# Block-causal attention with an RWKV channel mix: every PSUM use takes a pair of banks, the channel mix goes in pairs of blocks

## The chip, the cores and the metric

The kernel runs on one core of one Trainium2 chip. The metric is the device time of one execution in microseconds; lower is better. The engines named below are TensorE (PE, with its weight loads PEld), VectorE (DVE), ScalarE (ACT), GpSimd (POOL) and SyncE (SP). They work side by side, each through its own instructions in order, and wait for each other on semaphores.

## What is computed

Attention over 8 batches of 8 heads, 576 tokens and 64 columns per head, where a query block of 64 sees its own and earlier key blocks; then a channel mix over the 4608 tokens of 512 columns.

```python
scores = where(block_i >= block_j, q @ k.T / sqrt(64), -1e9)
x = softmax(scores) @ v                      # heads side by side: 8 x 576 x 512
x_prev = x shifted by one token
xk = mu_k * x + (1 - mu_k) * x_prev
xr = mu_r * x + (1 - mu_r) * x_prev
k = maximum(xk @ w_k, 0)                     # 512 -> 1024
v = (k * k) @ w_v                            # 1024 -> 512
out = sigmoid(xr @ w_r) * v                  # float32
```

The sigmoid is computed as a tanh: 0.5 * (1 + tanh(0.5 r)), with the 0.5 folded into w_v.

## The kernel before

The attention goes batch by batch. For each batch, `add_qk` loads q and k for four heads at a time and VectorE transposes them ("turn", L458); `add_unit` makes the scores of six units of up to 512 columns (TensorE L563; keys on partitions) into two pairs of PSUM banks, and ScalarE takes the exponential of each pair in one instruction of 1024 columns (L584). `add_av` multiplies with v: kind S sums the exponentials (L647), T, A and B are the products (L658); VectorE makes the reciprocals of the sums and normalizes into `xt` (L687, L695). `add_mix` forms xk and xr of the batch (differences on POOL, DVE or ACT, L778, L782; products on VectorE, L798, L802). Batch 0 goes in two parts of its own (`add_part`).

The channel mix goes by chunks of 512 tokens, nine in all. In chunk c, `add_pk` multiplies for one of eight column blocks jc of w_k (four matmuls of 512 columns, L834), then comes a relu into `kr` (ACT L847 or DVE L849) and a square into `k2` (ACT L856, DVE or POOL L858). `add_pr` does one of four token blocks of 128 with w_r (four matmuls, L873) and a tanh (ACT, L882). `add_pv` does one token block with w_v (eight matmuls, L903), VectorE forms (1 + tanh) * v as the output (L911), and SyncE stores 128 x 512 of it (L918). The first 192 tokens of chunk 0 go apart from its other 320.

Each of these steps is a task of a plan. `ORDER` lists the tasks by number, and that is the order in which they are issued, so the order on every engine; "+n" puts n filler matmuls ahead of a TensorE task (`unread`, L413). `PLACE` says with one letter each which engine takes a task that could go to several.

PSUM has eight banks of 512 float32 columns per partition. They are held as four tiles of two banks (`t_ps0` to `t_ps3`). Attention takes a whole tile (size 2); every k, r and v group takes one bank, that is half a tile (size 1). `take` chooses the half: first one whose neighbour is in use, then the one that was freed first in the order of issue:

```python
elif b["size"] == 1:
    at = min((ring[n ^ 1][1], s[0], n)
             for n, s in enumerate(ring) if s[1])[2]
```

Buffers behind the PSUM groups: four `kr`, four `t` and three `o`, each of 512 columns.

Of the kernel before, what the change touches and what calls it, by code (L numbers as in the profile page):

```python
# [61 lines left out]
"""  # L62

PLACE = (
    "SPSDSPADDDAAAAPAAPDDDPDPDPDPAAPPAPPDDADPAPPDPAPPDAPDPADAPPPDADAAAADDDA"
    "AAAAAPAPAPAPAPAPAPDPAAADAAAAAPAPAPAPAPAPAPDPAPAPAAAAAAADAAAPAAADAPADDA"
    "APAADDAAAAAADAAAAADADDADDPADAAAADDADAADPAAAPADADAPAPAAAAADDDDPAAAPDDAA"
    "DADAADDDADAADA")


class Plan:


    def __init__(self, rings):
        self.rings = rings
        self.slots = {n: [[i, True] for i in range(k)] for n, k in rings.items()}
        self.tasks = []
        self.issued = 0
# [925 lines left out]
```

## Time and profile before

| what | value |
|---|---|
| median of 3 runs | 299.59 us (299.56 to 302.61) |
| profiled execution: time, span | 299.6 us, 297.8 us |
| granted TensorE clock, mean | 0.966 |
| PE busy | 258.8 us (87%) |
| DVE busy | 190.6 us (64%) |
| ACT busy | 176.2 us (59%) |
| POOL busy | 74.5 us (25%) |
| chain that ended last: PE, DVE, ACT | 73%, 10%, 7% |

The span goes from the first to the last instruction of the profiled execution; its time is 1.8 us longer. Busy times of TensorE hold the matmuls' pipelined ends, so a run of matmuls counts some 0.2 us beyond its last start interval. The chain is the sequence of work that ended last: TensorE makes up three quarters of it, and the instructions that empty PSUM stand between its pieces. A timeline row gives start, length, engine, line, operation, tiles and how many instructions it merges; in brackets stands the engine's idle time ahead of it and whose end ended that.

### The profile page before, as it was taken

What the parts mean: (1) busy time and instruction counts of PE and PEld (TensorE: products, weight loads), DVE (VectorE), ACT (ScalarE), POOL (GpSimd) and SP (SyncE); (2) the same over time, 40 slices, a digit from 0 to 9 for tenths busy, and PEclk for the clock granted to TensorE, in tenths of its full rate; (3) what the DMA queues carried; (4) which work ended last, traced back from release to release, by engine and by line L of the source; (5) the groups of instructions that cost most, each with busy time, mean ns of one, the idle gap of its engine ahead of it and who ended that gap; (6) DMA issues with size and microseconds to landing.
All of it is one profiled execution on the core that took longest, in us unless ns stands there. A gap on an engine that the chain in (4) does not pass through costs nothing.

```text
span 297.8 us, 9076 instructions
## 1 busy us (share of the span) xinstructions
PE 258.8 (87%) x4056; PEld 133.5 (45%) x4056; DVE 190.6 (64%) x266; ACT 176.2 (59%) x255; POOL 74.5 (25%) x91
## 2 busy tenths in 40 slices
PE   8689489999998998998999889898988999886763
PEld 3356134753453445543544575454445644332322
DVE  0657860798787778969677768776855593452021
ACT  1077067688976787776658868866754754650101
POOL 0334320145568226313352002101030400200000
PEclk9979855999999999999999999999999999999999
DMA  7999999627999399729538600200111003001122
GB/s 167 220 210 188 194 255 267 118 34 111 212 223 206 50 237 206 133 69 235 85 53 175 155 4 2 108 35 4 37 73 37 2 0 141 2 1 51 56 78 98
DMA packets 49911, 33.75 MB, mean 113 GB/s; under 512 B 39248, under 2 KB 39504, under 8 KB 49872
## 3 DMA queue, kind: packets, MB, share of 16 engines
q1 hardware_dynamic: 44816, 22.75, 32.5%
q0 software_dynamic: 4896, 9.83, 19.8%
q10 hardware_dynamic: 160, 0.59, 0.8%
q8 instruction: 31, 0.51, 0.7%
q14 instruction: 8, 0.07, 0.1%
HBM read 33.56 MB, written 9.44 MB: 144 GB/s over the span
## 4 chain that ended last, share of the span: by engine, by line
PE 73%; DVE 10%; ACT 7%; issue 5%; DMA 3%; SPq 1%; POOL 0%; DVEq 0%; ACTq 0%; POOLq 0%
PE t_ps L834 21%; PE t_ps L903 20%; PE t_ps L873 10%; PE t_ps L563 9%; PE t_ps L658 6%; PE t_ps L413 4%; DVE t_o L911 4%; PE t_ps L647 3%; DMA t_lq<-in_q_dram 3%; ACT t_t L882 3%; ACT t_kr L847 2%; DVE t_qkt L458 2%; DVE t_kr L849 1%; ACT t_e L584 1%; DVE t_xt L695 1%
## 5 line engine op out<-in xcount | busy, mean ns | idle before, releaser
L584 ACT ACTIVATE t_e<-t_ps 128x1024 f16<-128x1024 f32 (+3 forms) x96 | 87.8, 973 | 33.4 <-PE t_ps L563 33.3
L834 PE MATMUL t_ps<-t_xk,WK 128*128 128x512 f16 (+5 forms) x416 | 69.0, 315 | 8.8 <-ACT t_kr L847 5.6
L903 PE MATMUL t_ps<-WV,t_k 128*128 128x512 f16 (+1 forms) x296 | 67.6, 373 | 9.0 <-DVE t_o L911 3.9
L834 PEld LDWEIGHTS <-WK 128*128 128x128 f16 x416 | 37.0, 98 | 36.2 <-issue 12.4
L847 ACT ACTIVATE t_kr<-t_ps 128x512 f32<-128x512 f32 (+2 forms) x61 | 31.8, 553 | 29.7 <-PE t_ps L834 17.1
L911 DVE SCALAR_TENSOR_TENSOR t_o<-t_t,t_ps 128x512 f32<-128x512 f32 (+1 forms) x37 | 24.2, 669 | 35.8 <-PE t_ps L903 26.0
L903 PEld LDWEIGHTS <-t_k 128*128 128x128 f16 x296 | 27.9, 97 | 42.8 <-issue 13.2
L858 POOL TENSOR_TENSOR t_k<-t_kr 128x512 f16<-128x512 f32 (+2 forms) x28 | 26.1, 944 | 78.1 <-DVE t_kr L849 45.3
L882 ACT ACTIVATE t_t<-t_ps 128x512 f32<-128x512 f32 x36 | 20.8, 598 | 39.6 <-PE t_ps L873 22.9
L563 PE MATMUL t_ps<-t_qkt 32*64 32x64 bf16 (+7 forms) x1328 | 40.0, 310 | 3.6 <-DVE t_qkt L458 2.9
L873 PE MATMUL t_ps<-WR,t_xr 128*128 128x512 f16 x144 | 36.1, 381 | 5.0 <-DVE t_o L911 4.3
L458 DVE STREAM_TRANSPOSE t_qkt<-t_nb 128x576 f32<-128x576 f32 x32 | 37.7, 1241 | 4.0 <-PE t_ps L563 2.2
L563 PEld LDWEIGHTS <-t_qkt 32*64 32x64 bf16 x1328 | 21.7, 111 | 27.3 <-issue 22.9
L849 DVE TENSOR_SCALAR t_kr<-t_ps 128x512 f32<-128x512 f32 (+2 forms) x19 | 12.0, 643 | 30.7 <-PE t_ps L834 17.9
L782 POOL TENSOR_TENSOR t_d<-t_xt 128x576 f32<-128x576 f32 (+2 forms) x14 | 16.6, 1188 | 56.6 <-DVE t_xr L802 21.9
L413 PE MATMUL t_ps<-identb 128*128 128x512 bf16 x72 | 22.6, 442 | 3.4 <-ACT t_e L584 1.9
L856 ACT ACTIVATE t_k<-t_kr 128x512 f16<-128x512 f32 (+2 forms) x33 | 18.9, 585 | 6.9 <-DVE t_kr L849 6.4
L873 PEld LDWEIGHTS <-t_xr 128*128 128x128 f16 x144 | 13.3, 98 | 20.6 <-issue 7.3
L802 DVE SCALAR_TENSOR_TENSOR t_xk<-t_d,MUK,t_xt 128x576 f16<-128x576 f32 (+2 forms) x26 | 21.4, 830 | 1.1 <-POOL t_d L782 1.0
L658 PE MATMUL t_ps<-t_e,t_vo 64*32 64x64 f16 (+7 forms) x1120 | 21.3, 284 | 0.8 <-issue 0.6
L695 DVE TENSOR_TENSOR t_xt<-t_ps,t_rt 128x1024 f32<-128x1024 f32 x14 | 17.0, 1222 | 6.4 <-PE t_ps L658 6.4
L802 DVE SCALAR_TENSOR_TENSOR t_xr<-t_d,MUR,t_xt 128x576 f16<-128x576 f32 (+2 forms) x26 | 19.7, 771 | 0.1
(43 smaller groups left out, 175.2 us busy)
## 6 DMA issues: line engine op xcount, KB each, us to landing
t_lv<-in_v_dram SPq DMA_DIRECT2D x32, 288.0 KB, 7.5
out_dram<-t_o SPq DMA_DIRECT2D x35, 256.0 KB, 2.2
t_nb<-in_k_dram POOLq DMA_DIRECT2D x14, 288.0 KB, 6.1
t_nb<-in_q_dram POOLq DMA_DIRECT2D x14, 288.0 KB, 6.5
t_lq<-in_moe_w_v_dram SPq DMA_DIRECT2D x4, 512.0 KB, 21.5
t_lq<-in_q_dram SPq DMA_DIRECT2D x4, 288.0 KB, 8.5
WK<-in_moe_w_k_dram POOLq DMA_DIRECT2D x4, 256.0 KB, 10.3
t_lq<-in_k_dram ACTq DMA_DIRECT2D x2, 288.0 KB, 5.3
```

The lines of the kernel that those rows point to most:

```text
L413: nc.tensor.matmul(dst, identb, identb[:, :].unsqueeze(1).to_broadcast([P, 4, P]), start=True, stop=True)
L458: nc.vector.transpose(new(qkt)[:, n, g].rearrange("p t e -> p (t e)").bitcast(FP).rearrange("p (r j) -> p j r", r=RW), new(nb)[:, :].bitca ...
L563: nc.tensor.matmul(new(ms[a // 2])[y * D:y * D + D, a % 2, col:col + n], qkt[rows, 1, g, t * D:t * D + D, f], qkt[rows, 0, g, q0:q0 + n, f ...
L584: nc.scalar.activation(new(e)[:, 2 * h:2 * h + 2, 0:w], new(ms[h])[:, :, 0:w], AF.Exp, scale=ISQ)
L658: nc.tensor.matmul(PA[o, u, HALF + f * D:HALF + f * D + D] if kind == "T" else PA[o, u, lo - D:lo - D + n], weight(b, u, c, t % JT, f), E[ ...
L802: e.scalar_tensor_tensor(dst, dt[:, 0, 0:W], (MUK1, MUR1)[n][:, cc:cc + 1], x, ALU.mult, ALU.add)
L834: nc.tensor.matmul(ps[:, a:a + n], WK[:, cc, jc * P:(jc + 1) * P], MIX[0][:, cc, at:at + n], start=(cc == 0), stop=(cc == CCn - 1))
L847: nc.scalar.activation(kt, ps, AF.Relu)
L873: nc.tensor.matmul(ps, MIX[1][:, cc, g % XW:g % XW + P], WR[:, cc], start=(cc == 0), stop=(cc == CCn - 1))
L882: nc.scalar.activation(new(tb), new(m), AF.Tanh, scale=0.5)
L903: nc.tensor.matmul(ps[:, 0:w], k2[:, jc, jt * P:(jt + 1) * P], WV[:, jc, cols], start=(jc == 0), stop=(jc == JCn - 1))
L911: nc.vector.scalar_tensor_tensor(new(o)[:, 0:w], new(tiles["tbf", c, jt])[:, cols], 1.0, new(m)[:, 0:w], ALU.add, ALU.mult)
```

## The change

Every PSUM use now takes a whole tile of two banks; `size`, `take` and `mark` go, and a task takes the free tile that was freed first in the order of issue. The channel mix goes in pairs: `add_pk` does two column blocks into the two banks of a tile (four blocks for the 192 tokens at the start), with one relu and one square of 1024 columns; `add_pr` does two token blocks with one tanh; `add_pv` does two token blocks with one output instruction and one store of 256 x 512. The very last pair is split into one block of 512 columns and two halves of 256. The matmuls are the same in number and shape. Buffers: three `kr`, two `t`, two `o`, each of 1024 columns. `ORDER` has 684 tasks instead of 897 and is a new table, with 70 fillers instead of 72; `PLACE` is new too. Tasks by kind and engine, counted in the plan:

| kind | before | change |
|---|---|---|
| relu | 61 ACT, 19 DVE | 26 ACT, 12 DVE |
| square | 33 ACT, 19 DVE, 28 POOL | 18 ACT, 9 DVE, 11 POOL |
| tanh | 36 ACT | 18 ACT |
| output, store | 37, 37 | 20, 20 |
| difference of the mix | 10 ACT, 12 DVE, 14 POOL | 13 ACT, 11 DVE, 12 POOL |
| casts of q, k, v, w_v | 8 ACT, 7 DVE, 9 POOL | 10 ACT, 5 DVE, 9 POOL |

The core of the diff:

```diff
-    def take(self, b):
...
-        elif b["size"] == 1:
-            at = min((ring[n ^ 1][1], s[0], n)
-                     for n, s in enumerate(ring) if s[1])[2]
...
             if b["slot"] is None:
-                self.take(b)
+                ring = self.slots[b["ring"]]
+                at = min((s[0], n) for n, s in enumerate(ring) if s[1])[1]
+                ring[at][1] = False
+                b["slot"] = at
...
-             "rc": 2, "rt": 1, "d": 2, "xk": 2, "xr": 2, "kr": 4, "k2": 2,
-             "t": 4, "o": 3, "ps": 8}
+             "rc": 2, "rt": 1, "d": 2, "xk": 2, "xr": 2, "kr": 3, "k2": 2,
+             "t": 2, "o": 2, "ps": 4}
...
-    def add_pk(c, jc, lo, hi):
-        m, kr = plan.buf("ps", 1), plan.buf("kr")
+    def add_pk(c, j0, lo, hi):
+        w = hi - lo
+        per = CH // w
+        m, kr = plan.buf("ps"), plan.buf("kr")
+        jcs = range(j0, j0 + 2 * per)
...
+            for jc in jcs:
+                x, y = divmod(jc - j0, per)
+                for a, n, at in parts:
+                    for cc in range(CCn):
+                        nc.tensor.matmul(
+                            ps[:, x, y * w + a:y * w + a + n],
+                            WK[:, cc, jc * P:(jc + 1) * P],
+                            MIX[0][:, cc, at:at + n],
+                            start=(cc == 0), stop=(cc == CCn - 1))
...
-            kt, ps = new(kr)[:, 0:w], new(m)[:, 0:w]
+            kt = new(kr)[:, 0:2 * per * w].rearrange("p (x j) -> p x j", x=2)
+            ps = new(m)[:, :, 0:per * w]
...
-    def add_pr(c, jt):
-        m = plan.buf("ps", 1)
+    def add_pr(c, j0):
+        m = plan.buf("ps")
+            for x in range(2):
+                g = (c * CH + (j0 + x) * P) % XW
+                for cc in range(CCn):
+                    nc.tensor.matmul(
+                        ps[:, x], MIX[1][:, cc, g:g + P], WR[:, cc],
+                        start=(cc == 0), stop=(cc == CCn - 1))
...
-    def add_pv(c, jt):
-        halves = 2 if (c, jt) == (NCH - 1, 3) else 1
+    def add_pv(c, j0):
+        last = (c, j0) == (NCH - 1, 2)
+        for x0, nx, c0, w in ([(0, 1, 0, CH), (1, 1, 0, 256), (1, 1, 256, 256)]
+                              if last else [(0, 2, 0, CH)]):
+            m, o = plan.buf("ps"), plan.buf("o")
...
                 nc.vector.scalar_tensor_tensor(
-                    new(o)[:, 0:w], new(tiles["tbf", c, jt])[:, cols],
-                    1.0, new(m)[:, 0:w], ALU.add, ALU.mult)
+                    new(o)[:, xs, cols], new(tb)[:, xs, cols],
+                    1.0, new(m)[:, xs, cols], ALU.add, ALU.mult)
```

What the new tables do to the engines is seen in the built order. The first place is the end of the program on VectorE: the output instructions (L911, in the change L893), the last relus (L849, now L823) and squares (L858, now L833); `t_o`, `t_t` and `t_kr` are their buffers. Before:

```order
L849 TENSOR_SCALAR t_kr3_141<-t_ps0_151 128x512
L911 SCALAR_TENSOR_TENSOR t_o1_149<-t_t0_144,t_ps0_151 128x512
L911 SCALAR_TENSOR_TENSOR t_o2_150<-t_t1_145,t_ps0_151 128x512
L911 SCALAR_TENSOR_TENSOR t_o0_148<-t_t2_146,t_ps0_151 128x512
L911 SCALAR_TENSOR_TENSOR t_o1_149<-t_t3_147,t_ps0_151 128x512
L911 SCALAR_TENSOR_TENSOR t_o2_150<-t_t0_144,t_ps0_151 128x512
L911 SCALAR_TENSOR_TENSOR t_o0_148<-t_t1_145,t_ps0_151 128x512
L911 SCALAR_TENSOR_TENSOR t_o1_149<-t_t2_146,t_ps0_151 128x512
L911 SCALAR_TENSOR_TENSOR t_o2_150<-t_t3_147,t_ps1_152 128x256
```

In the change:

```order
L823 TENSOR_SCALAR t_kr2_140<-t_ps3_150 128x1024
L833 TENSOR_TENSOR t_k20_141<-t_kr2_140 128x1024
L833 TENSOR_TENSOR t_k20_141<-t_kr1_139 128x1024
L893 SCALAR_TENSOR_TENSOR t_o0_145<-t_t0_143,t_ps1_148 128x1024
L893 SCALAR_TENSOR_TENSOR t_o1_146<-t_t1_144,t_ps2_149 128x1024
L893 SCALAR_TENSOR_TENSOR t_o0_145<-t_t0_143,t_ps3_150 128x1024
L893 SCALAR_TENSOR_TENSOR t_o1_146<-t_t1_144,t_ps2_149 128x512
L893 SCALAR_TENSOR_TENSOR t_o0_145<-t_t1_144,t_ps0_147 128x256
L893 SCALAR_TENSOR_TENSOR t_o1_146<-t_t1_144,t_ps3_150 128x256
```

Eight reads in a row of the one tile `t_ps0` have become reads that go round `t_ps1`, `t_ps2`, `t_ps3` and `t_ps0`.

The second place is ScalarE around chunk 6 of the channel mix and the last scores of batch 7: exponentials (L584, now L550), relus (L847, now L821), squares (L856, now L831) and tanhs (L882, now L859). Before:

```order
L584 ACTIVATE t_e2_124<-t_ps0_151 128x2x320
L882 ACTIVATE t_t1_145<-t_ps3_154 128x512
L882 ACTIVATE t_t2_146<-t_ps3_154 128x512
L847 ACTIVATE t_kr0_138<-t_ps0_151 128x512
L856 ACTIVATE t_k20_142<-t_kr0_138 128x512
L847 ACTIVATE t_kr1_139<-t_ps0_151 128x512
L847 ACTIVATE t_kr2_140<-t_ps3_154 128x512
L847 ACTIVATE t_kr0_138<-t_ps3_154 128x512
```

In the change:

```order
L550 ACTIVATE t_e1_123<-t_ps1_148 128x1024
L550 ACTIVATE t_e1_123<-t_ps2_149 128x1024
L550 ACTIVATE t_e2_124<-t_ps1_148 128x2x320
L550 ACTIVATE t_e2_124<-t_ps2_149 128x2x320
L859 ACTIVATE t_t1_144<-t_ps3_150 128x1024
L821 ACTIVATE t_kr0_138<-t_ps1_148 128x1024
L831 ACTIVATE t_k20_141<-t_kr0_138 128x1024
```

Reads of one tile by two tanhs or two relus in a row have become one read of the whole tile, and the next read is of another tile.

## Rows read from the trace of the kernel before

**Rows 1.** Stretches: from:to and length, busy us by engine, PEclk, DMA, GB/s

```profile
0.00:57.30 57.30, 46.02 (x791) 24.33 (x792) 28.76 (x55) 26.63 (x36) 14.53 (x26) 0.82 1.04 207
57.30:237.87 180.57, 167.91 (x3066) 89.43 (x3066) 137.75 (x176) 130.72 (x188) 56.74 (x62) 1.00 0.51 104
237.87:297.80 59.93, 44.84 (x206) 19.70 (x204) 24.12 (x36) 18.86 (x32) 3.21 (x4) 1.00 0.14 53
...
40.00:50.00 10.00, 10.00 (x148) 4.40 (x142) 1.80 (x4) 8.25 (x9) 2.14 (x2) 0.50 1.08 275
```

**Rows 2.** Timeline 272 to 286 us, TensorE and ScalarE around the handovers

```profile
272.54 1.02 PE L873 MATMUL t_ps<-WR,t_xr 128*128 128x512 f16 x4 [0.78 <-DVE t_o L911]
...
274.34 1.02 PE L873 MATMUL t_ps<-WR,t_xr 128*128 128x512 f16 x4 [0.78 <-DVE t_o L911]
...
275.40 0.60 ACT L882 ACTIVATE t_t<-t_ps 128x512 f32<-128x512 f32 x1 [4.86 <-PE t_ps L873]
276.05 1.89 PE L903 MATMUL t_ps<-WV,t_k 128*128 128x512 f16 x8 [0.69 <-ACT t_t L882]
...
278.62 1.89 PE L903 MATMUL t_ps<-WV,t_k 128*128 128x512 f16 x8 [0.69 <-ACT t_t L882]
...
281.29 1.89 PE L903 MATMUL t_ps<-WV,t_k 128*128 128x512 f16 x8 [0.78 <-DVE t_o L911]
...
283.96 1.89 PE L903 MATMUL t_ps<-WV,t_k 128*128 128x512 f16 x8 [0.78 <-DVE t_o L911]
```

**Rows 3.** Timeline 228 to 235 us: two k groups and the relu behind

```profile
228.24 1.92 PE L834 MATMUL t_ps<-t_xk,WK 128*128 128x384 f16 x16
...
230.19 0.60 ACT L847 ACTIVATE t_kr<-t_ps 128x512 f32<-128x512 f32 x1 [3.45 <-PE t_ps L834]
...
230.84 3.65 PE L834 MATMUL t_ps<-t_xk,WK 128*128 128x384 f16 x32 [0.69 <-ACT t_kr L847]
```

**Rows 4.** TensorE's waits, 237.87 to 297.8: us, times, longest

```profile
PE t_ps L903 <- ACT t_t L882: 2.7, 4, 0.7
PE t_ps L873 <- DVE t_o L911: 2.4, 3, 0.8
```

**Rows 5.** TensorE's waits, 57.3 to 237.87

```profile
PE t_ps L834 <- ACT t_kr L847: 3.7, 5, 0.9
PE t_ps L873 <- DVE t_o L911: 2.0, 3, 1.0
```

**Rows 6.** Timeline: an unbroken run of k matmuls, and the last matmuls

```profile
253.32 6.20 PE L834 MATMUL t_ps<-t_xk,WK 128*128 128x512 f16 x28 [0.69 <-ACT t_t L882]
...
292.84 1.03 PE L903 MATMUL t_ps<-WV,t_k 128*128 128x256 f16 x8 [0.68 <-ACT t_t L882]
```

**Rows 7.** The tail's matmuls by line (L834, L903, L873): PE busy (count), PEld

```profile
237.87:294.00 56.13, 14.78 (x64) 6.24 (x64) 1.00 0.14 52
237.87:294.00 56.13, 22.51 (x104) 10.12 (x104) 1.00 0.14 52
237.87:294.00 56.13, 8.85 (x36) 3.34 (x36) 1.00 0.14 52
```

**Rows 8.** Groups by form: busy us, mean ns of one, idle before

```profile
L584 ACT ACTIVATE t_e<-t_ps 128x1024 f16<-128x1024 f32 x78 | 75.7, 1026 | 18.9 <-PE t_ps L563 18.8
L847 ACT ACTIVATE t_kr<-t_ps 128x512 f32<-128x512 f32 x48 | 27.2, 598 | 22.9 <-PE t_ps L834 16.0 <-DVE t_kr L849 6.4 <-PE t_ps L873 0.2
L911 DVE SCALAR_TENSOR_TENSOR t_o<-t_t,t_ps 128x512 f32<-128x512 f32 x35 | 23.4, 684 | 33.7 <-PE t_ps L903 23.8 <-PE t_ps L873 5.0 <-ACT t_t L882 3.5
L695 DVE TENSOR_TENSOR t_xt<-t_ps,t_rt 128x1024 f32<-128x1024 f32 x14 | 17.0, 1222 | 6.4 <-PE t_ps L658 6.4
```

**Rows 9.** Timeline: ScalarE instructions back to back, merged

```profile
213.62 1.94 ACT L584 ACTIVATE t_e<-t_ps 128x1024 f16<-128x1024 f32 x2
...
235.78 1.58 ACT L847 ACTIVATE t_kr<-t_ps 128x512 f32<-128x512 f32 x3 [0.52 <-PE t_ps L834]
```

**Rows 10.** The chain that ended last, in the start

```profile
30.33 4.43 issue
```

More of the change, by code (lines that the diff above doesn't have):

```diff
@@ L87, in add, with buf @@
         return t
-    def buf(self, ring, size=0):
-        return {"ring": ring, "left": 0, "slot": None, "size": size}
-    def take(self, b):
-        ring = self.slots[b["ring"]]
-        if b["size"] == 2:
-            at = min((max(ring[2 * p][0], ring[2 * p + 1][0]), p)
-                     for p in range(len(ring) // 2)
-                     if ring[2 * p][1] and ring[2 * p + 1][1])[1]
-        elif b["size"] == 1:
-            at = min((ring[n ^ 1][1], s[0], n)
-                     for n, s in enumerate(ring) if s[1])[2]
-        else:
-            at = min((s[0], n) for n, s in enumerate(ring) if s[1])[1]
-        b["slot"] = at
-        self.mark(b, None)
-    def mark(self, b, when):
-        ring, at = self.slots[b["ring"]], b["slot"]
-        for n in (2 * at, 2 * at + 1) if b["size"] == 2 else (at,):
-            ring[n] = [ring[n][0] if when is None else when, when is not None]
+    def buf(self, ring):
+        return {"ring": ring, "left": 0, "slot": None}
     def issue(self, t):
@@ L200 @@
              for ring, n in RINGS.items() if ring in SHAPES
-             for at in range(n // 2 if ring == "ps" else n)}
+             for at in range(n)}
     def new(buf):
-        at = buf["slot"]
-        if buf["size"] == 1:
-            return slots[buf["ring"], at // 2][:, at % 2]
-        return slots[buf["ring"], at]
+        return slots[buf["ring"], buf["slot"]]
     identb = consts.tile([P, P], BF)
@@ L551, in add_unit @@
         w = max(col + n for col, _, _, n in pieces)
-        ms = [plan.buf("ps", 2) for _ in range(2)]
+        ms = [plan.buf("ps") for _ in range(2)]
         def fn(eng, me, heads):
@@ L631, in add_av @@
         vals = [cast["v", b, m] for m in range(2)]
-        m = {kind: plan.buf("ps", 2) for kind in "SAB"}
+        m = {kind: plan.buf("ps") for kind in "SAB"}
         m["T"] = m["S"]
@@ L849, in relu @@
                 nc.vector.tensor_scalar_max(kt, ps, 0.0)
-        r = add(f"relu {c} {jc} {lo}", ("ACT", "DVE"), relu, [t],
-                uses=[kr, m], kind="relu", cols=w)
+        r = add(f"relu {c} {j0} {lo}", ("ACT", "DVE"), relu, [t],
+                uses=[kr, m], kind="relu", cols=2 * per * w)
         def sq(eng, me):
-            KR, dst = new(kr)[:, 0:w], new(k2b)[:, jc, lo:hi]
+            KR = new(kr)[:, 0:2 * per * w].rearrange("p (j t) -> p j t", t=w)
+            dst = new(k2b)[:, j0:j0 + 2 * per, lo:hi]
             if eng == "ACT":
@@ L869, in fn @@
+    def add_pr(c, j0):
+        m = plan.buf("ps")
+        tb = tiles["tbf", c, j0] = plan.buf("t")
         def fn(eng, me):
             ps = new(m)
-            unread(me, ps)
-            for cc in range(CCn):
-                nc.tensor.matmul(
-                    ps, MIX[1][:, cc, g % XW:g % XW + P], WR[:, cc],
-                    start=(cc == 0), stop=(cc == CCn - 1))
-        deps, bufs = mixed_in(1, g, g + P)
-        t = add(f"pr {c} {jt}", ("PE",), fn,
+            unread(me, ps[:, 0])
+            for x in range(2):
[4 more added lines that the diff above has]
+                        start=(cc == 0), stop=(cc == CCn - 1))
+        g = c * CH + j0 * P
+        deps, bufs = mixed_in(1, g, g + 2 * P)
+        t = add(f"pr {c} {j0}", ("PE",), fn,
@@ L878, in add_pr @@
                 deps + [cast["w", "r", i] for i in range(2)],
[L879 removed]
+                uses=[m, tb] + bufs, kind="mm", cols=[CH] * CCn * 2)
         def tanh(eng, me):
             nc.scalar.activation(new(tb), new(m), AF.Tanh, scale=0.5)
[L883 to L884 removed]
+        act["t", c, j0] = add(f"tanh {c} {j0}", ("ACT",), tanh, [t],
+                              uses=[m, tb], kind="tanh", cols=2 * CH)
@@ L886, with fn @@
     o2 = out.rearrange("b s c -> (b s) c")
[L888 to L906 removed]
+    def add_pv(c, j0):
+        last = (c, j0) == (NCH - 1, 2)
+        k2s = [t for lo, hi in SUBS.get(c, [(0, CH)])
+               if lo < j0 * P + 2 * P and hi > j0 * P
+               for t in act["k2", c, lo]]
+        tb = tiles["tbf", c, j0]
+        for x0, nx, c0, w in ([(0, 1, 0, CH), (1, 1, 0, 256), (1, 1, 256, 256)]
+                              if last else [(0, 2, 0, CH)]):
+            m, o = plan.buf("ps"), plan.buf("o")
+            xs = slice(x0, x0 + nx)
+            cols = slice(c0, c0 + w)
+            def fn(eng, me, xs=xs, cols=cols, m=m):
+                ps, k2 = new(m), new(tiles["k2b", c])
+                unread(me, ps[:, 0])
+                for x in range(xs.start, xs.stop):
+                    at = (j0 + x) * P
+                    for jc in range(JCn):
+                        nc.tensor.matmul(
+                            ps[:, x, cols], k2[:, jc, at:at + P],
+                            WV[:, jc, cols], start=(jc == 0),
+                            stop=(jc == JCn - 1))
+            t = add(f"pv {c} {j0} {2 * x0 + c0}", ("PE",), fn,
@@ L914, in add_pv @@
-            t = add(f"o {c} {jt} {half}", ("DVE",), ov, [t, act["t", c, jt]],
-                    uses=[o, m, tiles["tbf", c, jt]], kind="o", cols=w)
-            def store(eng, me, cols=cols, o=o):
-                nc.sync.dma_start(o2[g:g + P, cols], new(o)[:, 0:w])
-            add(f"store {c} {jt} {half}", ("SP",), store, [t], uses=[o],
-                kind="st", kb=P * w * 4 / 1024)
-    wbuf = plan.buf("ps", 1)
-    add("spare", ("PE",), lambda eng, me: unread(me, new(wbuf)), uses=[wbuf], kind="spare", cols=[])
+                    new(o)[:, xs, cols], new(tb)[:, xs, cols],
@@ new lines, in ov, with store @@
+                    1.0, new(m)[:, xs, cols], ALU.add, ALU.mult)
+            t = add(f"o {c} {j0} {2 * x0 + c0}", ("DVE",), ov,
+                    [t, act["t", c, j0]], uses=[o, m, tb], kind="o",
+                    cols=w * nx)
+            def store(eng, me, xs=xs, cols=cols, o=o):
+                g = c * CH + j0 * P
+                nc.sync.dma_start(
+                    o2[g:g + 2 * P].rearrange(
+                        "(x p) j -> p x j", p=P)[:, xs, cols],
+                    new(o)[:, xs, cols])
@@ L925 @@
+            add(f"store {c} {j0} {2 * x0 + c0}", ("SP",), store, [t],
+                uses=[o], kind="st", kb=P * w * nx * 4 / 1024)
+    wbuf = plan.buf("ps")
+    add("spare", ("PE",), lambda eng, me: unread(me, new(wbuf)[:, 0]), uses=[wbuf],
+        kind="spare", cols=[])
     mu_ready = []
@@ L965 @@
         for lo, hi in SUBS.get(c, [(0, CH)]):
-            for jc in range(JCn):
-                add_pk(c, jc, lo, hi)
-        for jt in range(4):
-            add_pr(c, jt)
-        for jt in range(4):
-            add_pv(c, jt)
+            for j0 in range(0, JCn, 2 * (CH // (hi - lo))):
+                add_pk(c, j0, lo, hi)
+        for j0 in (0, 2):
+            add_pr(c, j0)
+        for j0 in (0, 2):
+            add_pv(c, j0)
     for t in plan.order():
```

66 lines of the change are left out of this document (19 added, 47 removed), and 81 rows, old and new, of the table ORDER.

## The prediction

> **What bounds the kernel now.** I read the stretches first, then TensorE's waits in each, then the order of time around those waits. [rows 1] cuts the span of 297.8 us at two places: 57.30 us, where the attention product of batch 1 starts, and 237.87 us, where the last attention product (batch 7, kind B) ends. Behind 57.30 the granted clock is 1.00, so what is lost there is idle time. Middle: TensorE is busy 167.91 of 180.57 us (93%), VectorE 137.75 (76%), ScalarE 130.72 (72%). Tail (channel mix alone): TensorE 44.84 of 59.93 us, VectorE 24.12, ScalarE 18.86. So TensorE bounds both, and in the tail it is idle 15.1 us while both evacuating engines are idle more than half the time: nothing is short of throughput, something hands over badly.
>
> [rows 2] shows what. Matmul group, evacuation, matmul group follow each other without overlap: TensorE stands 0.69 us behind a tanh, or 0.78 us behind an output instruction, and starts right after it. With more than one free bank an evacuation should run under the next group. The ScalarE row at 275.40 tells why it doesn't: this tanh reads the first of two r groups, which was done about 273.56 us (272.54 + 1.02), but it starts at 275.40, when the second group, in the neighbour bank, ends (274.34 + 1.02 = 275.36). The reader waits for the write to the other half of its pair, and the next write to the pair waits for the reader. [rows 3] shows the same in the middle: two k groups (16 matmuls) run to 230.16, then the relu of the first of them starts at 230.19, and TensorE waits for it. So a pair of banks is one thing to the waits, although the planner hands out halves, and it likes to fill up a pair of which the other half is in use.
>
> One handover costs, start to start less the matmuls themselves: 512-wide matmuls take (6.20 − 1.89)/(28 − 8) = 0.2155 us each [rows 2, 6], eight 1.72 us. With a tanh between, 278.62 − 276.05 = 2.57, a loss of 0.85; with an output between, 283.96 − 281.29 = 2.67, a loss of 0.95.
>
> How many there are: going along the built order, tile by tile, I count the groups that cannot start before an evacuation that itself cannot start before TensorE's directly preceding group has ended. Before there are 24: 1 ahead of 57.30 us, 8 in the middle, 15 in the tail. The trace has exactly 15 waits of TensorE for evacuations in the tail, 11.1 us of recorded idle ([rows 4] gives seven of them), and 19 in the middle, 11.8 us ([rows 5] gives eight of them). In the change the same count is 0: the nearest such distance is two groups, mostly three or four.
>
> **The change, part by part.**
>
> *Tail, −13 us.* The matmuls between 237.87 and the last are 64 + 104 + 36 = 204 [rows 7]; 16 of the second kind are 256 wide, 8 of which take 1.03 us against 1.89 [rows 6, 2], so about 0.11 us each. Work: 188 × 0.2155 + 16 × 0.11 = 42.3 us. It took 293.87 − 237.87 = 56.0 (last matmul 292.84 + 1.03, [rows 6]); 13.7 us are stall. In the change a k, r or v group owns a pair, and the order of the tail goes round the four pairs, so an evacuation has three groups of 1.72 us or more to finish in, over 5 us. Its price rises: a 1024-wide ScalarE read of PSUM takes 1.026 against 0.598 us for 512, a 1024-wide VectorE product with one PSUM operand 1.222 against 0.684 [rows 8]. Both lie well under 5 us. What stays is the first fill, where the first k groups of chunk 7 need the mixed rows of batch 7 on VectorE: 1.22 for the last normalization, six products and an output, some 7.5 us, behind two v pairs and an r pair of 8.6 us. I leave 0.7 us of stall. The last output still goes out in two 256-wide halves; both ends stay as they are. Bounds: 0 (the stall has another cause) to 13.7.
>
> *Middle, −8 us.* The 8 serial handovers at 0.85 us are 6.8 us. Of the other 11 waits (11.8 us less about 8 × 0.7, some 6 us) I take 1.2 us, since they come from evacuations that are late on their own queue, and with pairs the scores still take two of four pairs at a time. Bounds: 0, and all the idle time, 180.57 − 167.91 = 12.7 us. What could be late next: a v pair now holds TensorE 3.45 us (16 × 0.2155) before the next scores, so exponentials come in lumps.
>
> *Fewer, wider instructions, 0.* Relu, square, tanh and output fall from 80, 80, 36 and 37 to 38, 38, 18 and 20. What one saves must be read back to back: three relus take 1.58 us, that is 0.49 us for each further one; two 1024-wide exponentials 1.94, 0.92 for the second [rows 9]. A pair so saves 2 × 0.49 − 0.92 = 0.06 us; for about 30 pairs on ScalarE that is 2 us, on VectorE about as little, on engines with over 40 us to spare in the middle. The table also puts three more pairs of difference scalings and two more V casts on ScalarE, eight instructions of about the microsecond that 1024 columns take there [rows 8]. Nothing of it is on the path; it would cost those few us if ScalarE became the bound. Stores double in size and halve in number; only the last ones can show, and they are unchanged in width.
>
> *Start, 0.* TensorE's clock is 0.50 in 40 to 50 us with TensorE busy 10.00 of 10 us and ScalarE 8.25 [rows 1], after a gap of 4.43 us in the middle of one attention product [rows 10]. The new order puts 12 fillers instead of 9 ahead of that product, and the weight loads a little earlier. At full clock the exponentials would bound, worth 10 − 8.25 = 1.75 us; a second gap of the kind would cost 4.4. I take 0 between −1.75 and +4.4.
>
> Sum: 297.8 − 13 − 8 + 0 = 276.8 us of span. The profiled execution took 299.6 for its span of 297.8, the median of the runs is 299.59, so 1.8 us are added: 278.6, rounded to 278.5.
>
> **The rivals.**
>
> A: *only the tail gains.* The middle keeps its length, because each batch runs in lockstep: VectorE needs the sums of the attention product, TensorE the normalized rows, and wide groups come later to a queue that is three quarters full [rows 1]. For it: of the 19 waits there 11 aren't of the serial kind. Against it: 8 are. Time: 299.6 − 13 = 286.6.
>
> B: *pairs are too coarse, slower.* In the middle 12 v pairs stand between scores. Each holds TensorE 1.72 us longer at a stretch than one bank's group did; if the exponentials are then late by as much each time, 12 × 1.72 = 20.6 us are added, and 299.6 − 13 + 20.6 = 307. It decides where ScalarE has no slack in a batch. Against it speaks its 72%, that is 50 us of idle time in the middle [rows 1]. The Trainium skill speaks for it: Perfetto Trace Analysis, Matmul Optimizations, says that all 8 PSUM banks should be in use for parallelism, and four units are fewer than eight. By that rule the loss would be in the middle, where most is in flight; the rows of before show eight banks that wait as four.
>
> C: *the change does not remove the wait.* If the waits came from the evacuating engine alone and not from the neighbour bank, 15 handovers of 0.9 us in the tail would become about 12, each longer by 0.43 us (1.026 − 0.598), 12 × 1.3 = 16 us instead of 13.7, and the time would be about 300. Against it: the tanh at 275.40, which started 1.8 us after its own group was done with ScalarE idle 4.86 us [rows 2]. The skill's PSUM — Partial Sum Buffer, in its summary, advises to read one bank while matmuls write a different one, guarded by bank; with such guards the handover of [rows 2] would not exist. The trace disagrees for this kernel: the guard is the pair.
>
> D: *more than the sum.* If the middle gives all 12.7 us and the start its 1.75, 297.8 − 13.7 − 12.7 − 1.75 + 1.8 = 271.5; of each 0.85 us, 0.85 − 0.69 = 0.16 are not in the recorded idle, which could add 3 us over some 20 handovers: 268.
>
> **How the numbers follow.** Chances: the forecast (272 to 284) 0.50; A 0.25 (284 to 290); D 0.13 (266 to 272); C, or another loss that eats the gain, 0.06; B 0.06. For the range I leave out C, B and a little of D: 268 to 290, about 0.83. A measurement of this kernel can tell about 1% (3 us) from no change. Faster by more than that are the forecast, A and D with a small part of C: 0.89; within 1%: 0.05; slower: 0.06.
>
> **What would show it.** Tail right: from the last B product to the end of the last matmul some 43 us (the r group at its head now earlier), TensorE's list of waits there nearly empty, relu, tanh and output starting while TensorE runs. Middle right: waits of TensorE for relu, tanh and output below 5 us, batches that follow each other faster. Wide instructions right: ScalarE's 1024-wide relu and tanh near 1.03 us, VectorE's output near 1.22. Wrong: TensorE waiting 1 us and more for wide reads (C), exponentials' idle time behind the scores grown by over 10 us (B), a clock below 1.00 behind 60 us, or a second gap in the start.

## The result and the profile after

The changed kernel takes 277.06 us (median of 4 runs, 274.74 to 277.94) beside 299.73 us for the kernel before: a ratio of 0.921, 95% interval 0.913 to 0.929. The profiled execution took 277.94 us, its span is 276.2 us (297.8 before). Over all their runs here the change lies between 270.6 and 277.9 us and the kernel before between 293.6 and 302.9, in part for a reason that stands in the last section.

Busy time by engine, from the page of the changed kernel; TensorE is busy 93% of the span (87% before):

```profile
PE 255.6 (93%) x4054; PEld 134.2 (49%) x4054; DVE 187.5 (68%) x229; ACT 173.9 (63%) x195; POOL 61.8 (22%) x72
```

The span of the changed kernel in four stretches (columns as in [rows 1]): up to the sum S of batch 1, up to the sum S of batch 7, up to the end of the last attention product, and the tail:

```profile
0.00:54.12 54.12, 44.09 (x729) 23.14 (x730) 27.62 (x51) 26.44 (x33) 13.74 (x25) 0.84 1.05 211
54.12:225.22 171.10, 164.03 (x2889) 86.87 (x2888) 132.10 (x149) 126.84 (x141) 46.93 (x46) 0.98 0.54 112
225.22:231.15 5.93, 5.93 (x238) 4.75 (x238) 4.55 (x7) 3.11 (x3) 0.00 (x0) 1.00 0.03 6
231.15:276.20 45.05, 41.56 (x200) 19.44 (x200) 23.24 (x25) 17.53 (x19) 1.14 (x1) 0.99 0.19 70
```

The same stretches of the kernel before, which [rows 1] cuts elsewhere:

```profile
0.00:54.15 54.15, 43.34 (x717) 22.13 (x718) 25.77 (x49) 24.88 (x31) 14.53 (x26) 0.81 1.06 210
54.15:226.87 172.72, 160.26 (x2925) 84.33 (x2924) 134.51 (x173) 126.96 (x184) 53.73 (x59) 1.00 0.54 111
226.87:237.87 11.00, 10.31 (x229) 7.31 (x214) 6.24 (x9) 5.51 (x10) 3.01 (x3) 1.00 0.01 3
```

The start is the same to 0.03 us. From there to the end of the last product it is 177.03 us in place of 183.72 (−6.7), and the tail is 45.05 in place of 59.93 (−14.9). Together that is the whole difference of the spans, 21.6 us.

The tail answers to [rows 2, 4, 6]. Its timeline on TensorE (start, length, engine, line, operation, tiles, count; idle ahead would stand in brackets):

```profile
231.08 7.08 PE L883 MATMUL t_ps<-WV,t_k 128*128 128x512 f16 x32
237.99 1.89 PE L849 MATMUL t_ps<-WR,t_xr 128*128 128x512 f16 x8
239.72 12.25 PE L806 MATMUL t_ps<-t_xk,WK 128*128 128x512 f16 x56
...
269.07 3.64 PE L883 MATMUL t_ps<-WV,t_k 128*128 128x512 f16 x24
```

No row has a bracket: from the last product to 272.71 us TensorE doesn't stand once. TensorE's waits over the whole span (us, times, longest) tell the same of the middle, beside [rows 5]:

```profile
PE t_ps L708 <- issue: 4.1, 1, 4.1
PE t_ps L529 <- issue: 3.8, 1, 3.8
...
PE t_ps L624 <- issue: 2.5, 1, 2.5
...
PE t_ps L379 <- DVE t_xt L661: 0.5, 1, 0.5
PE t_ps L379 <- ACT t_kr L821: 0.3, 1, 0.3
```

No relu, tanh or output holds up a matmul of the channel mix (L806, L849, L883) any more. What is new is "issue" in the middle, 6.3 us in two waits where before had 0.6 us in one:

```profile
93.36 0.63 PE L529 MATMUL t_ps<-t_qkt 32*64 32x448 bf16 x21
97.81 0.25 PE L529 MATMUL t_ps<-t_qkt 32*64 32x64 bf16 x11 [3.81 <-issue]
...
121.81 1.37 PE L624 MATMUL t_ps<-t_e,t_vo 64*32 64x512 f16 x65
125.69 0.25 PE L624 MATMUL t_ps<-t_e,t_vo 64*32 64x64 f16 x7 [2.52 <-issue]
```

Each stands inside one score group or one product, where no operand and no pair of banks changes hands. The wide instructions, beside [rows 8] (groups: busy us, mean ns | idle before):

```profile
L550 ACT ACTIVATE t_e<-t_ps 128x1024 f16<-128x1024 f32 (+3 forms) x96 | 87.9, 971 | 36.5 <-PE t_ps L529 36.4
L821 ACT ACTIVATE t_kr<-t_ps 128x1024 f32<-128x1024 f32 (+1 forms) x26 | 25.4, 977 | 25.9 <-PE t_ps L806 25.7
L893 DVE SCALAR_TENSOR_TENSOR t_o<-t_t,t_ps 128x1024 f32<-128x1024 f32 (+2 forms) x20 | 22.2, 1112 | 22.0 <-PE t_ps L883 15.4
L859 ACT ACTIVATE t_t<-t_ps 128x1024 f32<-128x1024 f32 x18 | 18.4, 1028 | 16.2 <-PE t_ps L849 16.2
```

### The profile page after: what moved, and what is told of

Read it like the earlier page. It is cut to its first block, busy times and chain, and to the rows that moved or that the text cites. A ratio compares the mean times of both kernels' runs of the same rounds, so it can differ in the third digit from the quotient of the medians.

```text
span 276.2 us, 8911 instructions
## 1 busy us (share of the span) xinstructions
PE 255.6 (93%) x4054; PEld 134.2 (49%) x4054; DVE 187.5 (68%) x229; ACT 173.9 (63%) x195; POOL 61.8 (22%) x72
## 4 chain that ended last, share of the span: by engine, by line
PE 86%; issue 4%; DMA 3%; ACT 3%; DVE 2%; SPq 1%; DVEq 0%; ACTq 0%
PE t_ps L806 23%; PE t_ps L883 23%; PE t_ps L529 12%; PE t_ps L849 12%; PE t_ps L624 7%; PE t_ps L379 4%; PE t_ps L613 3%; DMA t_lq<-in_q_dram 3%; ACT t_e L550 2%; PE t_ps L708 1%; DVE t_xt L661 1%; SPq L414 1%; ACT L365 0%; DVE t_qkt L424 0%; PE t_ps L688 0%
## 5 line engine op out<-in xcount | busy, mean ns | idle before, releaser
L550 ACT ACTIVATE t_e<-t_ps 128x1024 f16<-128x1024 f32 (+3 forms) x96 | 87.9, 971 | 36.5 <-PE t_ps L529 36.4
L806 PE MATMUL t_ps<-t_xk,WK 128*128 128x512 f16 (+5 forms) x416 | 69.2, 322 | 0.0
L883 PE MATMUL t_ps<-WV,t_k 128*128 128x512 f16 (+1 forms) x296 | 64.9, 374 | 0.0
L806 PEld LDWEIGHTS <-WK 128*128 128x128 f16 x416 | 37.8, 101 | 25.2 <-issue 2.0
L883 PEld LDWEIGHTS <-t_k 128*128 128x128 f16 x296 | 28.0, 98 | 32.6 <-issue 1.3
L821 ACT ACTIVATE t_kr<-t_ps 128x1024 f32<-128x1024 f32 (+1 forms) x26 | 25.4, 977 | 25.9 <-PE t_ps L806 25.7
L893 DVE SCALAR_TENSOR_TENSOR t_o<-t_t,t_ps 128x1024 f32<-128x1024 f32 (+2 forms) x20 | 22.2, 1112 | 22.0 <-PE t_ps L883 15.4
L849 PE MATMUL t_ps<-WR,t_xr 128*128 128x512 f16 x144 | 35.5, 393 | 0.0
L859 ACT ACTIVATE t_t<-t_ps 128x1024 f32<-128x1024 f32 x18 | 18.4, 1028 | 16.2 <-PE t_ps L849 16.2
L833 POOL TENSOR_TENSOR t_k<-t_kr 128x1024 f16<-128x1024 f32 (+1 forms) x11 | 18.2, 1659 | 44.6 <-ACT t_kr L821 27.0
L823 DVE TENSOR_SCALAR t_kr<-t_ps 128x1024 f32<-128x1024 f32 (+1 forms) x12 | 14.2, 1180 | 16.0 <-PE t_ps L806 16.0
L748 POOL TENSOR_TENSOR t_d<-t_xt 128x576 f32<-128x576 f32 (+2 forms) x12 | 13.5, 1126 | 43.3 <-DVE t_xt L720 14.4
L624 PE MATMUL t_ps<-t_e,t_vo 64*32 64x512 f16 (+7 forms) x1120 | 20.8, 284 | 2.5 <-issue 2.5
L849 PEld LDWEIGHTS <-t_xr 128*128 128x128 f16 x144 | 13.6, 100 | 16.4 <-issue 2.0
L624 PEld LDWEIGHTS <-t_vo 64*32 64x32 f16 x1120 | 14.5, 92 | 11.4 <-issue 7.0
L404 POOL DMA_DIRECT2D t_nb<-in_k_dram x14 | 8.0, 571 | 51.1 <-DVE t_qkt L424 50.3
L831 ACT ACTIVATE t_k<-t_kr 128x1024 f16<-128x1024 f32 (+1 forms) x18 | 18.6, 1036 | 0.4
```

What stands on the lines that cost most here:

```text
L550: nc.scalar.activation(new(e)[:, 2 * h:2 * h + 2, 0:w], new(ms[h])[:, :, 0:w], AF.Exp, scale=ISQ)
L624: nc.tensor.matmul(PA[o, u, HALF + f * D:HALF + f * D + D] if kind == "T" else PA[o, u, lo - D:lo - D + n], weight(b, u, c, t % JT, f), E[ ...
L806: nc.tensor.matmul(ps[:, x, y * w + a:y * w + a + n], WK[:, cc, jc * P:(jc + 1) * P], MIX[0][:, cc, at:at + n], start=(cc == 0), stop=(cc ...
L821: nc.scalar.activation(kt, ps, AF.Relu)
L831: nc.scalar.activation(dst, KR, AF.Square)
L849: nc.tensor.matmul(ps[:, x], MIX[1][:, cc, g:g + P], WR[:, cc], start=(cc == 0), stop=(cc == CCn - 1))
```

## The experiments

In the rows of the experiments line numbers are shifted by the edits: by 12 from the kernel before in the first two, and by −5 to +6 from the changed kernel in the others.

**The old kernel, other halves in the tail.** Only the choice of the half is changed, by a list with one number for each use (a half of eight, or for a whole tile a pair of four); order, widths and engines stay. Serial handovers, counted as in the prediction, fall from 24 to 9, the nine ahead of the tail staying.

```diff
+HALVES_OF_PS = """
+0 1 2 3 0 1 2 3 0 6 0 3 1 0 2 6 0 1 2 3 2 3 2 0 3 1 2 0 3 1 4 5 0 1 4 6 1 7 6 7 0 2 6 7 4 5
...
+"""
...
-        if b["size"] == 2:
+        if b["ring"] == "ps":
+            at = int(next(self.ps))
+        elif b["size"] == 2:
```

> The kernel before with its order, its instructions and its widths; only which half of which pair a use takes is another in the tail (behind the last attention product), read from a list, so that the tail's single-bank groups go round the pairs. Serial handovers (a group that cannot start before an evacuation which waits for the directly preceding group): 9 instead of 24, none in the tail. Theory H (a pair is one thing to the waits, and the handover is the cost): 13 to 14 us less than before, 286 to 287 us, with nearly no wait of TensorE in the tail. Rival W (the gain comes from fewer and wider evacuations): no change, 299 to 300 us. Rival O (it comes from the new order): no change either.

Measured: 286.86 us (284.09 to 289.51), ratio 0.964, interval 0.952 to 0.977, beside 300.03 for before on that chip. The tail in its trace, from the end of the last product (238.87) to the end of the span (285.3), is 46.4 us, 13.5 less than before, and TensorE's list of waits there is empty. One of its rows, beside [rows 6], is forty v matmuls in one run where before stood after every eight:

```profile
269.42 8.80 PE L915 MATMUL t_ps<-WV,t_k 128*128 128x512 f16 x40
```

So the tail's 13 us were the neighbour bank, and it takes neither the new order nor the wide instructions to get them. That is also the test of rival C: by the Trainium skill (PSUM — Partial Sum Buffer, summary) one bank may be read while matmuls write another, guarded by bank. In this kernel the guard is the pair, since moving groups to other pairs is what freed them. No run gives each bank a tile of its own, so whether the pair counts as one because the program holds it as one tile stays open.

**The same for the whole program.** Serial handovers fall from 24 to 1; the edit is the one above with a list for every use.

```diff
 HALVES_OF_PS = """
-0 1 2 3 0 1 2 3 0 6 0 3 1 0 2 6 0 1 2 3 2 3 2 0 3 1 2 0 3 1 4 5 0 1 4 6 1 7 6 7 0 2 6 7 4 5
+0 0 1 2 3 0 1 2 3 4 0 3 2 1 0 6 2 1 0 3 0 3 2 1 0 3 2 1 0 3 4 2 0 1 3 4 3 0 1 2 2 0 2 3 4 0
...
```

> As the run with other halves in the tail, but the list is another for the whole program: 1 serial handover instead of 24 (scores of batch 2), all with the order, instructions and widths of before. Theory H: the tail's 13 to 14 us and 7 to 9 us in the middle, 277 to 281 us. Rival W and rival O: no change, 299 to 300 us; if both H and O have a part, 282 to 290 us.

Measured: 288.45 us (286.61 to 289.62), ratio 0.972, 0.963 to 0.982: nothing gained over the run before. Part of that is the start, which the list changes too: the sum S of batch 1 comes at 56.93 us, against 53.97 with the tail alone. From there to the sum S of batch 7 it takes 172.39 us, against 173.90 with the tail alone and 172.72 before (171.10 in the change, with 6.3 us of "issue" in it). TensorE's waits there, "issue" left out, fell only from 11.8 us in 20 to 9.5 in 16, and stand behind other work now:

```profile
PE t_ps L575 <- ACT t_e L596: 1.8, 3, 0.7
PE t_ps L885 <- ACT t_e L596: 1.6, 2, 1.2
PE t_ps L846 <- DVE t_xt L707: 1.4, 1, 1.4
PE t_ps L846 <- ACT t_t L894: 1.1, 2, 0.7
PE t_ps L915 <- ACT t_e L596: 1.0, 1, 1.0
```

In the old order this list of halves doesn't buy off the middle's handovers: for 6.4 of the 9.5 us the pair that a group is sent to instead is held by an exponential or a normalization. No other list was tried. By this one, what the change gains in the middle comes from its order, or from its order and pairs together.

**The change with its evacuations split.** Each relu, square, tanh and output goes as two of half the width; pairs and order stay.

```diff
-                nc.scalar.activation(kt, ps, AF.Relu)
+            for x in range(2):
+                nc.scalar.activation(kt[:, x], ps[:, x], AF.Relu)
```

> The changed kernel, but relu, square, tanh and output of a pair are two instructions of half the width each, one behind the other on the same engine; pairs, order and buffers stay. Theory H: the evacuations lie beside matmuls, so 277 to 279 us. Rival W: most of the gain is lost, 288 us or more.

Measured: 275.61 us (272.96 to 278.4), ratio 0.921, 0.908 to 0.934, that of the change. Its trace takes 220.7 us from the sum S of batch 1 to the end, against 222.1. Two tanhs of 606 ns are no dearer to the path than one of 1028, so the wide instructions give and cost nothing:

```profile
L822 ACT ACTIVATE t_kr<-t_ps 128x512 f32<-128x512 f32 x44 | 23.9, 598 | 18.4 <-PE t_ps L806 18.3
L863 ACT ACTIVATE t_t<-t_ps 128x512 f32<-128x512 f32 x36 | 19.5, 606 | 15.8 <-PE t_ps L852 9.3 <-DVE t_o L899 6.5
```

**The change, its tail on the pair freed last.** Of the tail's 20 groups 18 now stand two groups behind the previous use of their pair; in the change 19 stand four or more behind.

```diff
-                at = min((s[0], n) for n, s in enumerate(ring) if s[1])[1]
+                last = b["ring"] == "ps" and self.issued >= 615
+                at = (max if last else min)(
+                    (s[0], n) for n, s in enumerate(ring) if s[1])[1]
```

> The changed kernel, but in the tail (from the second group behind the last attention product) a use takes the free pair that was freed last instead of the one freed first. Nearest distance of an evacuation that a group waits for: two groups instead of mostly four; no serial handover. Theory H (only a distance of one costs): 277 us within 1. Rival D (it takes three or four groups of slack): each of some 18 groups of the tail waits 0.2 to 0.5 us, 281 to 286 us.

Measured: 275.59 us (274.51 to 276.6), ratio 0.929, 0.918 to 0.940. In the tail two waits appear, one of 0.21 us behind a normalization for the first group and one of 0.26 us behind a relu on VectorE:

```profile
248.01 1.89 PE L808 MATMUL t_ps<-t_xk,WK 128*128 128x512 f16 x8 [0.26 <-DVE t_kr L825]
```

Otherwise one group of 1.9 us between two uses of a pair covers an evacuation there.

**The change, its middle on the pair freed last.** The same edit from step 150 to step 614 of the order. With the two score groups of a unit counted as one block, 6 blocks of the middle stand at distance one and nearly 90 at two; in the change none and some 30, of which 23 are scores.

```diff
-                at = min((s[0], n) for n, s in enumerate(ring) if s[1])[1]
+                last = b["ring"] == "ps" and 150 <= self.issued < 615
+                at = (max if last else min)(
+                    (s[0], n) for n, s in enumerate(ring) if s[1])[1]
```

> The changed kernel where from the 150th to the 614th step of the order a tile takes the pair freed last, as before the tail in the old kernel more often happened: six matmul blocks of the channel mix (pr 0 2, pk 1 0, pk 1 2, pr 1 0, pr 1 2, pv 2 0) now follow their pair's own previous user at once, and 96 in place of 40 stand at distance two. H (the middle's gain is made of handovers, 0.85 us each): 6 x 0.85 = 5 us more, 281 to 283. O (the middle's gain is the new order and grouping, which leaves ScalarE's line short): no more than 1 us, 276 to 278.

Measured: 301.2 us (296.71 to 303.35), ratio to before 1.014, 1.004 to 1.025. Both theories missed by 18 us and more: this choice of pairs alone eats the whole gain, and the time is about that of before. TensorE waits 28.1 us for evacuations between the sums S of batches 1 and 7, in 36 places (1.0 us in 3 in the change), most of them at distance two:

```profile
196.95 0.66 PE L531 MATMUL t_ps<-t_qkt 32*64 32x448 bf16 x32
198.33 1.89 PE L851 MATMUL t_ps<-WR,t_xr 128*128 128x512 f16 x8 [0.72 <-DVE t_o L895]
200.15 0.66 PE L531 MATMUL t_ps<-t_qkt 32*64 32x384 bf16 x32
201.33 1.89 PE L851 MATMUL t_ps<-WR,t_xr 128*128 128x512 f16 x8 [0.52 <-ACT t_t L861]
```

The group in between is a score group of 0.66 us, not 1.9 as in the tail, and the tanh or output takes over 1 us. So it isn't the number of groups between two uses of a pair that counts but their time, and it must cover the evacuation and whatever stands ahead of it on its engine: at 130.64 us TensorE waits 1.20 us for an exponential that a square of 1.06 us on ScalarE has held up. Between the sums S of batches 1 and 7 this run takes 193.06 us, against 172.72 before and 171.10 in the change. With the second experiment: the new pairs tried on the old order do nothing for the middle, the new order with badly chosen pairs is worse there than before, and of the versions here only the change's order with its pairs removes the waits. Which feature of the order does it (fewer and longer blocks, or where the scores stand between them) wasn't separated.

**What "issue" is: a shift of 8 matmuls.** The start wait [rows 10] stands in both kernels behind the 479th matmul of the program; the two new ones behind the 1503rd and the 1887th. These are 479 plus 8 and 11 times 128. The counts, from the stretch up to each wait (TensorE's busy us, then the count in parentheses):

```profile
0.00:31.60 31.60, 25.78 (x479) 13.90 (x480) 15.19 (x28) 14.59 (x18) 9.39 (x20) 0.95 1.05 202
0.00:94.10 94.10, 83.22 (x1503) 43.79 (x1504) 62.53 (x89) 60.01 (x70) 34.26 (x47) 0.91 0.97 190
0.00:123.30 123.30, 108.59 (x1887) 56.79 (x1888) 82.64 (x111) 78.52 (x90) 40.32 (x55) 0.92 0.90 176
```

The page of either kernel has a queue "instruction" with 31 packets and 0.51 MB, and 4054 matmuls over 128 are 31.7. The edit puts 8 more unread matmuls at the start, where TensorE waits for its first operands anyway:

```diff
-6 0+36 3 12 9 7 8 15 4 17
+6 0+44 3 12 9 7 8 15 4 17
```

> Asked here: what the waits that the trace calls issue are, in the changed kernel (4.07 us after 479 matmuls, 3.81 after 1503, 2.52 after 1887, counted from the program's first). The changed kernel with 44 unread matmuls at its very start instead of 36; they end before the first operands land (11.6 us against 15.1 before), so nothing later should shift in time. F (blocks of 128 matmuls with their weight loads are brought in by transfers that queue behind the loads): the waits stay at the counts 479, 1503 and 1887, so they fall 8 matmuls earlier in the work: after 147 of batch 0's products where it was 155, after 13 of the score group where it was 21, after 57 of the products where it was 65. P (something at that place of the work is awaited that the profile doesn't show): they stay behind 155, 21 and 65. Both: about the same time, 274 to 279 us.

Measured: 273.15 us in one run, a little under what was expected. In the timeline the waits moved by exactly the eight matmuls; 13 products are left behind the first where 5 were, and 19 of the score group where 11 were:

```profile
34.52 0.27 PE L708 MATMUL t_ps<-t_e,t_vo 64*32 64x128 f16 x13 [3.44 <-issue]
95.65 0.45 PE L529 MATMUL t_ps<-t_qkt 32*64 32x448 bf16 x19 [4.31 <-issue]
```

The third, behind 1887, is absent here; one of 0.81 us stands 128 matmuls later instead, and another of 1.40 us behind the 863rd, which is 479 plus 3 times 128. The place is a count of instructions, not a piece of work. The Trainium skill (Trainium Architecture — The Big Picture, The software stack) gives 64 bytes to an instruction. By that figure 0.51 MB over 31 packets is, as an estimate, 257 instructions a packet, about 128 matmuls and their weight loads.

**Fewer loads under the second wait.** The four q and k loads of batch 5 are issued behind the third difference of batch 2, at 97.0 to 98.6 us in place of 86.8 to 94.8.

```diff
-509 184 514 265 185 218 510 263 317 186 515 270 315 269 221 187 222 511 190
+509 184 514 265 185 218 510 263 186 515 270 269 221 187 222 511 190
...
-228 516 321 319 229 199 230 200 517 518 198 231 201 232 202 271 203 233 519
+228 516 229 199 230 200 517 518 198 231 201 232 202 271 203 317 315 321 319 233 519
```

> The changed kernel with the four q and k loads of batch 5 issued behind the third difference of batch 2 on POOL (about 99 us in place of 86.8, 87.8, 94.2 and 94.8); they are wanted at about 113 us. F (instruction blocks wait behind loads): with half the loads gone from 86 to 98 us, the 3.81 us wait after 1503 matmuls falls under 1.5, and the median by 2.5 to 5 us, to 272 to 275 (against 277). P (the wait belongs to the place, not to the loads): it stays at 3.4 to 3.9 us and the median at 277.

Measured: 268.1 us (266.73 to 269.8), ratio 0.901, 0.893 to 0.909. The wait behind 1503 fell from 3.81 to 1.55 us, at the same place:

```profile
93.60 0.25 PE L524 MATMUL t_ps<-t_qkt 32*64 32x64 bf16 x11 [1.55 <-issue]
```

So the wait depends on the loads, though it stayed a little over the 1.5 us that were forecast. The median fell by more than forecast. Part of that is the start: the sum S of batch 1 comes at 50.99 us in this trace, against 54.12 in the change, for the reason in the last section. From there to the end it is 217.0 us against 222.1. The version was run again, without a further edit, beside the change as it is on the same chip.

> The changed kernel itself once more, beside the two runs that follow on the same chip. Its median is expected within 274 to 279 us; whether the half clock behind the wait after 479 matmuls lasts 3 or 14 us (both were seen, 3.3 us apart at the sum S of batch 1) decides where in it a run falls.

> The version with batch 5's four q and k loads later, once more beside the change itself. F: 5 to 9 us under the change on the same chip, 266 to 271 us. If the first result was only a lucky start (the short half clock), no more than 1 us under it once runs with equal starts are compared.

Measured: the change 274.97 us (270.59 to 277.34), the later loads 269.13 (267.86 to 273.16): 5.8 us apart, within what was forecast. But a good part of it is again the start. Three of the four runs of the later loads have a mean granted clock of 0.987, and one of the change's; between these it is 267.86, 268.17 and 270.09 against 270.59 us. In the two traces the sum S of batch 1 comes at 54.39 us in the change and at 50.72 with the later loads, and from there to the end it takes 220.6 and 220.7 us. The wait behind 1503 in the two traces:

```profile
98.86 0.32 PE L529 MATMUL t_ps<-t_qkt 32*64 32x64 bf16 x11 [4.60 <-issue]
```
```profile
93.10 0.25 PE L524 MATMUL t_ps<-t_qkt 32*64 32x64 bf16 x11 [1.91 <-issue]
...
120.64 0.22 PE L619 MATMUL t_ps<-t_e,t_vo 64*32 64x64 f16 x7 [2.19 <-issue]
```

The first wait is shorter by 2.7 us, but the next, behind 1887, takes 2.19 us, against 1.41 in the change. That the later loads shorten the wait behind 1503 is shown twice; what they are worth in time is 5.1 us behind the start in one pair of traces and nothing in the other, and stays open.

**Also the loads under the third wait.** As above, and batch 5's turns on VectorE go behind the first half of batch 3's normalization, so that batch 6's loads come later.

```diff
-523 525 318 323 526 538 316 370 325 537 322 368 274 539 239 320 374 275 240 372 243
+523 525 323 526 538 325 537 274 539 239 275 240 243
...
-533 248 532 250
+533 248 318 316 322 320 370 368 374 372 532 250
```

> As the run before, and the four turns of batch 5 on DVE (and with them the four q and k loads of batch 6 that take their buffers) behind the norm of batch 3's first half, so that batch 6's loads come at about 126 us in place of 113 to 117. F: both waits, 3.81 and 2.52 us, fall under 1.5, and with the half clock behind them the median goes to 267 to 272. P: both stay, 277. If the turns come too late for DVE, scores of batch 5 wait instead, and the trace shows that wait on t_qkt.

Measured: 271.67 us (269.94 to 274.3), ratio 0.911, 0.904 to 0.917. There is no wait behind 1887 any more, as forecast, but the four turns (4.49 us on VectorE) now hold up the second half of batch 3's normalization, and scores wait for its pair:

```profile
129.46 1.08 PE L524 MATMUL t_ps<-t_qkt 32*64 32x384 bf16 x32 [2.94 <-DVE t_xt L656]
```

The transfer was moved by a detour over an engine that had no room there, and the gain went into another wait.

**And loads under the first wait.** On top of the later loads of batch 5: two q and k loads of batch 2 and half of batch 1's v load are issued some 14 us later.

```diff
-105 107 67 42+1 2 73 74+1 43 71 100 44 47 46 158 98 75 81+12 49 156 104 83 45
+105 67 42+1 2 73 74+1 43 71 100 44 47 46 98 75 81+12 49 104 83 45
...
-90 160 25 27 126 29 93 477 31 92
+90 160 158 156 25 27 126 29 93 477 31 107 92
```

> The same with three more loads moved away from the wait after 479 matmuls: the two q and k loads of batch 2 (issued at 28.1 and 29.4 us) behind the other two of that batch, about 42 us, and the second half of batch 1's v load behind the weight loads. F: the 4.0 us wait falls under 3, and the half clock behind it is short or absent in every run: 263 to 268 us. P: the wait stays 4.0 and the time at that of the run before. If batch 2's turns or batch 1's second v cast then wait for their loads, TensorE waits on t_qkt or t_vo between 42 and 66 us and the time is the same or worse.

Measured: 271.01 us (269.43 to 273.99), not under the 269.13 beside it, and three of the four runs have a mean granted clock of only 0.961 to 0.968, so by these the long half clock didn't go either. In the trace it is 217.2 us from the sum S of batch 1 to the end, as in the first trace of the later loads. The start wait stayed:

```profile
35.04 0.21 PE L703 MATMUL t_ps<-t_e,t_vo 64*32 64x64 f16 x5 [3.79 <-issue]
```

The DMA share from 26 to 30 us was 1.14 in this trace and 1.13 in the change's: these three loads weren't what filled the queues there. What does (the weights, issued on POOL at 19.9 to 23.0, are the nearest guess) wasn't tried.

## Why the prediction was right, point by point

**Total: right, partly by two errors that cancel.** 277.06 against 278.5, and 276.2 of span against 276.8.

**Tail, −13: right in mechanism and size.** From the last product to the end of the last matmul the prediction expected some 43 us; it is 272.71 − 231.15 = 41.6, all of it matmuls. The 0.7 us left for the first fill didn't occur, and four r matmuls (0.86 us) are done ahead of it. The upper bound of 13.7 stall is met in full, and the first experiment gets it on the old order by halves alone.

**Middle, −8: the sum nearly right (−6.7), its terms wrong.** Idle time of TensorE from the sum S of batch 1 to the last product was 183.72 − 160.26 − 10.31 = 13.15 us, of it 0.6 "issue"; after it is 177.03 − 164.03 − 5.93 = 7.07, of it 6.3 "issue". So waits for other engines fell by 11.8 us, not 8, nearly to the bound of 12.7; "issue" rose by 5.7; the matmuls themselves took 0.6 less, although the clock was halved for a while, as the next point shows. The step that failed is "Of the other 11 waits ... I take 1.2 us, since they come from evacuations that are late on their own queue": of all the waits for other engines three are left, 1.0 us together. And the step "8 serial handovers at 0.85" named only a part of the mechanism. Undone by themselves on the old order, by the one list tried, they gave no time that shows; with most blocks at distance two, which the prediction took as free ("the nearest such distance is two groups"), and six at one, the change's own order loses 24 us. Distance in time, not in groups, is what to count.

**The second "issue" wait: foreseen as a danger, in the wrong place.** The text expected one more of 4.4 us in the start, if anywhere. It came in the middle twice. Signs of it were in the trace of before: the wait behind 479 matmuls [rows 10], and a small one of 0.59 us behind the 2399th, 15 times 128 later. Behind each of the two new waits the granted clock also fell to 0.50 for some 3 us, with TensorE busy throughout (the change, from 98 and from 126 us):

```profile
98.00:100.00 2.00, 2.00 (x16) 0.74 (x7) 1.61 (x1) 1.88 (x2) 1.27 (x2) 0.54 0.90 164
...
126.00:128.00 2.00, 2.00 (x13) 1.32 (x13) 1.96 (x2) 0.00 (x0) 0.00 (x0) 0.50 0.89 135
```

The prediction's own signs of being wrong have "a clock below 1.00 behind 60 us" among them. It came, and the sum has no term for it; the larger fall of the other waits paid for it.

**Wide instructions, 0: right**, by the split run: 275.6 against 277.1. The prices of [rows 8] came out as read, 1028 ns for a tanh; the relu's and output's means, 977 and 1112, include narrower forms, and their 1024-wide forms alone take 1026 and 1218 ns.

**Start, 0: right in this execution**, the sum S of batch 1 at 54.12 against 54.15 us, both with a long stretch at the half clock. With the later loads, which change nothing up to there, it is at 50.7 and 51.0 us.

**Rivals.** A (only the tail, 286.6) is the first experiment to 0.3 us, but not the change. B (pairs too coarse): ScalarE's idle time behind scores is 36.4 us (the L550 row above; 33.3 in the same row of before), far from the 10 us more that it would need. So the loss that was drawn from the rule of the Trainium skill (Perfetto Trace Analysis, Matmul Optimizations: all 8 banks in use) didn't come: with four units 1.0 us of waits for other engines is left in the middle and none in the tail. The order in which the four are handed out counts far more, 24 us in the run with the pair freed last. C fell with the first experiment. D (268 to 271.5) didn't come. The later loads of batch 5 reach it, 268.1 and 269.1 us, the best version here, in part by the short half clock in the start.

## What to carry to other kernels

Find out what the waits treat as one buffer before counting how many there are, and hand out the one that has been free longest; count the rest between two uses in time, against the evacuation and the queue ahead of it. When a tighter schedule packs many short instructions together, look for idle time at regular instruction counts, and try whether bulk loads can be kept away from those stretches.
